# Two layers of Hedgehog linear attention and ReGLU on one core: the queries made token by token and normalised before the state products

## The chip, the cores and the metric

The kernel runs on one core of one Trainium2 chip. The metric is the device time in microseconds of one execution, as the median of the runs. The profile records one execution; its span runs from the first to the last recorded instruction.

## The reference

The input `x` has 2048 tokens of 512 features. Two layers with the same weights are applied, each an attention block A and an MLP block B, each with a layer norm without weights ahead of it and a residual behind it.

```
q, k, v = split(norm(x) @ wqkv)            # 32 heads of 16 features
p(u)    = concat(softmax(u @ w_phi), softmax(-u @ w_phi))   # 16 -> 32 features, per head
kv[h]   = sum over tokens of p(k)^T v ;  z[h] = sum over tokens of p(k)
o       = (p(q) @ kv) / (p(q) @ z + 1e-6)
x       = x + concat_heads(o) @ wo
x       = x + ((relu(norm(x) @ W_gate)) * (norm(x) @ W_up)) @ W_down      # F = 1376
```

There is no causal mask: every query needs the sums over all 2048 keys of its layer.

## The kernel before

**Tiles and stages.** The tokens form 16 tiles of 128. In each layer every tile passes through the keys (norm, transpose of the normalised tile `xn` to `xnTA`, the products K and V, the feature map of the key, and the products `kvz` that sum kv and z over all tiles). After the last tile, `build` copies the sums into `R`, the right-hand side of the state products. Then each tile passes through the attention (`attend`: state products `erq`, division, transpose of `o`, output projection `proj`, residual) and the MLP (`mlp`, in blocks of 1, 1, 2, 4, 4, 2 and 2 tiles in layer 0, and 1, 1, 2, 4, 4, 2, 1 and 1 in layer 1): gate and up products `G` and `Up` (L1068), the products of the last 96 columns `GU` (L1044), `hT` (L1076), `down` (L1101) and the residual (L1108). A finished tile of layer 0 goes on into the keys of layer 1 while other tiles are still in the MLP.

**The feature map.** The softmax over the 16 features of a head is the exponential, divided by its sum. `w_phi` is folded into the weights `Wk2` and `Wq2` at the start. For the keys, K is made token by token (128 tokens on the partitions, 512 columns); two exponentials on ACT (L852, of the value and of its negative) fill `ek`, DVE sums 64 groups of 16 (`sk`, L860), ACT makes 1/sum as exp(-ln(sum)) (L867, L870), and two halves of 512 columns are multiplied by it, on POOL or DVE (`phiK`, L879).

**The queries.** They are made feature by feature. `queries` (from L933) multiplies four tiles at once with the features on the partitions (L937), so that `Eq`, the two exponentials on ACT (L941), is already in the form that a state product needs as weights. They are not divided by their softmax sums. Instead `R` has 18 columns for each of 8 heads: 16 for kv, one for z and one of ones, masked by head. A product of 128 feature rows with 144 columns (L955) gives numerators, denominators and softmax sums; a tile needs 8 of them, in groups of 3, 3 and 2, each group in one of the two PSUM buffers of pool `q`. The copies `N` and `DS` (helper `evac`, L752 on ACT or L753 on DVE) take them out of PSUM. DVE then makes, for the softmax of the value and of the negative together: `m` (L971, L973) and its reciprocal (L975), the weights `w` (L977), the weighted numerators `pr` (L980) and their sum `o` (L985).

**From `o` to the residual.** `turn` transposes `o`, for the first two tiles of a layer on PE with a copy on ACT or DVE, for the others by a DMA transpose that SP issues (L787). Then follow `proj` (L992) and the residual sum in `X` (L997, L1001).

**The order of the work.** The order on every engine is fixed when the program is built. Each `op` is a group of instructions with an engine, a cost and a due time. `plan` is a list scheduler with modelled costs, buffers and a model of the SBUF port that DVE and POOL share. The due times (`DUE`) and the engine of the operations that can run on either of two (`PLACE`) are tables that a search has found. A buffer pool (`pool`, `psum`) has a fixed number of tiles, and an `op` that takes a buffer waits until one is free. SP issues nearly all DMAs, in its own queue order: the loads, the transposes of `xn`, `o` and `hr`, and the stores. PE gets filler products (`idle`, L746) while it would otherwise be idle near the start.

Of the kernel before, what the change touches and what calls it, by code (L numbers as in the profile page):

```python
# [8 lines left out]
P = 128  # L9
# [14 lines left out]
GE = HB * (DH + 2)  # L24
# [197 lines left out]

def dma(nbytes):
    return 530, 2000 + nbytes / RATE


class K:
# [9 lines left out]
    "1101000110000001001100001000100000000000010001111000011000010001110001000000000000011100100010111111"  # L237
    "1111000010110100000100000010000001100000011001011000011111100010000100001101010000001001111011010000"
    "1111100110100000010110000100000010100000010011011010100001000001001010001111110011001101111011000111"
    "1"  # L240
# [4 lines left out]
PAIRN, PAIRK = 4, T  # L245
# [5 lines left out]
    124840698555718, 124252925051631, 124840698555715, 125332623046249, 125332623046237, 125332623044945,  # L251
    124563716811943, 124651474002544, 125330408190868, 125332623046304, 124563716811957, 126266507667699,
    125634454115563, 126229628066192, 121775727240306, 126167001450013, 126167001450460, 127129188121561,
    127129188120464, 127094235901023, 126466639653490, 130976565015723, 126315242830809, 126026073780216,
    127094235902555, 127129188121381, 126296162928321, 126296162928067, 124164240787164, 125426364192401,
    125402334135098, 125572680463274, 125519371767392, 125974726071829, 125750504763376, 125579757280012,
    125111116517781, 125262546662859, 123870973169851, 125479091639646, 125519634893654, 125402750569735,
    125720420032606, 126315242829367, 126115429498044, 125777194724969, 125402334135128, 125288327727618,
    125426364192382, 125079834957741, 125262546664085, 125297196294117, 125083742970748, 125572680463271,
    125682458895960, 125340531910116, 125650771760537, 124924227899641, 125375805988896, 125375805988747,  # L260
    125222585690632, 124164240787379, 125079834952887, 125682458896453, 125073457285470, 124441555417783,
    125262546664362, 124559450906168, 125312265963603, 125309490505260, 125650771760388, 125521196029889,
    125302414876135, 125288971855969, 125302414876075, 125319036718893, 125310924577113, 125301244472799,
    125319889098234, 125304622980711, 124441555417022, 124696086271192, 125037102060107, 125289095968268,
    125310342882178, 125097433264852, 123938863413234, 125098635011495, 125302414877679, 125298443103361,
    125302414877834, 125345179807080, 125281974922696, 125170893464912, 125310924577844, 125298773455122,
    124760528650159, 125079834956090, 124164240787032, 125519634912639, 125297196294120, 125289095970570,
    125112530384860, 124947956071454, 125087041208877, 125295339242047, 125295339242044, 125310342881683,
    125302414876836, 125563590222055, 124550413597701, 125170893460583, 125310439811694, 125310924578485,
    125310342891023, 125079834956128, 125059086062919, 125340531910042, 125288971857093, 124938480631522,  # L270
    125016964293686, 125288327733509, 125223398503866, 125345179804453, 125223398503371, 125223398503413,
    128002429020973, 125310342881575, 125004873625443, 125004873624115, 125304250990101, 125307858833262,
    126406478372943, 124715538660738, 125381551257299, 125298773455119, 125309931740009, 125034120871986,
    125223398503145, 124934003878247, 124920547621783, 125117660356287, 125304250989589, 125381551258296,
    125724846491348, 125381551257440, 125381551255756, 124974964922671, 125098650067446, 125291692659804,
    125289095968030, 125289095968469, 125345179805242, 125288327732492, 125098635010687, 125281974923160,
    125307858833059, 125223398502787, 125307858834522, 125140858237361, 126040889629027, 125223398503832,
    125364446854524, 125252231261123, 125381551257841, 125304250990712, 125381551257935, 125172912230709,
    124370185364736, 125108599924050, 125310339518705, 125302251176246, 125291692659817, 116464344164560,
    124922363544296, 125116688267329, 125108599923765, 125310109452139, 125303189236999, 125098650066178,  # L280
    125111066291136, 125026249417504, 125310339519068, 125302251175868, 125301748943397, 125307858834419,
    125262656080157, 125307858833334, 125307858831723, 125281974922936, 125016007547146, 125096908962168,
    125140858236352, 126184070097670, 126789461067573, 124985972327150, 126493631750672, 125298443105832,
    125108599921161, 125095405692172, 124194527561572, 123915330190996, 125076395401661, 125296253501352,
    125034337760696, 125310144379949, 125172912227871, 124207139224249, 123569728375339, 125298628392740,
    125302384093186, 125034337760404, 125310109456339, 125302384093798, 124931075024483, 125294295865377,
    125294295865373, 125302251176101, 125315738277133, 125311054768224, 126406478373023, 125172912230494,
    125096908962530, 125251794872554, 124920547622585, 125303189240357, 125098650068694, 119253338445520,
    125310144376109, 124936451836160, 123979775168383, 123985197582245, 125308558845483, 125268086740942,
    125296661283390, 125310109454666, 125308302113579, 124976494725716, 125154886386050, 125154886386047,  # L290
    125310339518837, 125310339520186, 125311054773229, 115427298652791, 125028606409972, 125308302117330,
    124740066372422, 125309837287326, 124971491447171, 125390463209015, 125414317459497, 124998168317548,
    125310257912136, 125310339399315, 123124172544908, 125030291594481, 125098650066121, 125251794874681,
    125098650067377, 118590723041837, 125302384093189, 118558518521843, 119253338445444, 125315738276049,
    106461658784164, 94447193084223, 125174401625687, 125154442634399, 124740066371701, 125309837288789,
    124971491447250, 125700597007401, 125308302114021, 125724451257015, 125310339520700, 125310339519418,
    125311054772244, 106461658774504, 124207139226908, 125192403773820, 124998168316146, 125311054772195,
# [308 lines left out]
def kernel(  # L606
# [11 lines left out]
    def new(name, shape, dt=BF16):  # L618
        return sb.tile([P] + shape, dt, name=name)
# [600 lines left out]
```

## Time and profile before

| | |
|---|---|
| median of 3 runs | 383.95 us (383.95 to 384.48) |
| span of the profiled execution | 382.0 us, 7622 instructions |
| the profiled execution's own time | not given apart from its span; the median of the runs is 1.95 us above the span |
| granted TensorE clock | 1.00 in every stretch |
| PE, DVE, ACT, POOL busy | 371.5, 311.1, 215.0, 41.9 us |
| state products L955 | 256 of 128x144, 27.5 us busy |
| copies `N` and `DS` | 59 each on ACT (38.4 us), 37 each on DVE (25.0 us) |
| `m`, `m`, reciprocal, `w`, `pr`, `o` on DVE | 32 each: 6.8, 6.6, 10.9, 6.8, 21.8, 13.2 us |
| key sums `sk` on DVE | 32, 38.6 us, 1210 ns each |
| `phiK` | 38 halves on POOL (1102 ns), 26 on DVE (703 ns) |
| DMA transposes on SP | 101, landing 2.3 to 3.4 us after the issue in the median |

How to read it. Busy times of PE overlap, since a matmul is counted from its start to its modelled end, while the next one has started; the spacing of a run of matmuls in the chain of waits is their true rate. The chain of waits is followed back from the last instruction: each line has a start, a length and what ran, with a tile name and a source line. Busy time by stretches lists PE, PEld (weight loads), DVE, ACT, POOL, each with its number of instructions, then the granted clock, the share of the DMA engines and GB/s. In the timeline a line has a start, a length, the engine, the source line, the operation and the tiles, and in brackets the idle time ahead of it and what ended it.

### The profile page before, as it was taken

Reading aid. Unit: us, or ns where it says so; the run is one execution under the profiler, and the core shown is the slowest. Engines: PE = TensorE matmul, PEld = TensorE weight load, DVE = VectorE, ACT = ScalarE, POOL = GpSimd, SP = SyncE. Lnnn points to the kernel's source line nnn. Section 1 sums busy time; section 2 is a strip of 40 time slices with the busy share of each in tenths; the row PEclk is TensorE's granted clock in tenths of the full one; section 3 lists DMA queues with packets and bytes.
Section 4 is the critical chain, followed back from the end, with each engine's and each line's share of the span. In section 5 each row is a group of like instructions: output and inputs, shape, how many; then the busy total and the mean of one; then the engine's idle time right before and its main releaser. Section 6 shows DMA issues by size and latency. Waiting matters only on the chain.

```text
span 382.0 us, 7622 instructions
## 1 busy us (share of the span) xinstructions
PE 371.5 (97%) x2787; PEld 224.4 (59%) x2832; DVE 311.1 (81%) x798; ACT 215.0 (56%) x554; POOL 41.9 (11%) x44
## 2 busy tenths in 40 slices
PE   7999998999989999999999999999999999999996
PEld 4545456967545445554656654696855544467575
DVE  7999999999999989983694677999998976763334
ACT  6999989636445316772455679984526412243040
POOL 0276710000200000230020124000000000000000
PEclk9999999999999999999999999999999999999999
DMA  8497720222221321211200100013322221020110
GB/s 232 122 205 219 188 89 2 52 58 62 57 56 41 44 54 40 45 23 27 45 6 15 22 8 1 2 36 70 77 44 70 57 56 56 14 62 16 41 50 29
DMA packets 60869, 22.83 MB, mean 60 GB/s; under 512 B 52672, under 2 KB 59808, under 8 KB 60832
## 3 DMA queue, kind: packets, MB, share of 16 engines
q1 hardware_dynamic: 60416, 21.95, 24.9%
q8 instruction: 22, 0.36, 0.4%
q10 hardware_dynamic: 416, 0.39, 0.4%
q14 instruction: 15, 0.12, 0.1%
HBM read 7.91 MB, written 2.10 MB: 26 GB/s over the span
## 4 chain that ended last, share of the span: by engine, by line
PE 77%; DVE 17%; DMA 2%; issue 2%; ACT 1%; DVEq 0%
PE b L1068 31%; PE b L1101 17%; PE b L855 5%; PE b L849 5%; PE b L992 5%; PE b L937 5%; PE q L955 3%; PE b L1044 2%; PE q L896 2%; DMA xnTA<-xn 2%; DVE pr L980 1%; DVE bstA L810 1%; DVE bstB L810 1%; DVE sk L860 1%; DVE N L753 1%
## 5 line engine op out<-in xcount | busy, mean ns | idle before, releaser
L1068 PE MATMUL b<-xnTB,wgu 128*128 128x128 bf16 (+2 forms) x1191 | 152.3, 279 | 0.5
L1068 PEld LDWEIGHTS <-wgu 128*128 128x128 bf16 x1200 | 97.7, 98 | 42.5
L1072 ACT ACTIVATE gu<-b 128x512 bf16<-128x512 f32 (+1 forms) x83 | 48.0, 584 | 63.7 <-PE b L1068 61.3
L1101 PE MATMUL b<-wd,hT 128*128 128x512 bf16 (+3 forms) x349 | 82.3, 372 | 0.7
L879 POOL TENSOR_TENSOR phiK<-ek,sk 128x512 bf16<-128x512 bf16 x38 | 41.2, 1102 | 192.3 <-ACT sk L870 164.1
L1101 PEld LDWEIGHTS <-hT 128*128 128x128 bf16 (+1 forms) x363 | 34.7, 98 | 33.9 <-DVE hT L1076 0.2
L1076 DVE TENSOR_TENSOR hT<-gu 128x512 bf16<-128x512 bf16 (+1 forms) x83 | 34.0, 414 | 15.4 <-ACT gu L752 14.2
L1108 DVE SCALAR_TENSOR_TENSOR X<-b,rsB,X 128x512 bf16<-128x512 f32 (+1 forms) x33 | 23.7, 729 | 23.8 <-PE b L1101 23.8
L752 ACT CAST gu<-b 128x512 bf16<-128x512 f32 (+1 forms) x50 | 28.4, 570 | 24.0 <-PE b L1068 20.4
L860 DVE TENSOR_REDUCE sk<-ek 128x64 f32<-128x1024 bf16 x32 | 38.6, 1210 | 2.7 <-ACT ek L852 2.3
L852 ACT ACTIVATE ek<-b 128x512 bf16<-128x512 f32 x64 | 36.0, 616 | 8.3 <-PE b L849 8.1
L941 ACT ACTIVATE Eq<-b 128x512 bf16<-128x512 f32 x64 | 37.3, 629 | 3.3 <-PE b L937 3.1
L752 ACT CAST N<-q 128x384 bf16<-128x384 f32 (+1 forms) x59 | 26.1, 464 | 12.4 <-PE q L955 6.7
L855 PE MATMUL b<-wv,xnTA 128*128 128x512 bf16 x123 | 31.9, 379 | 0.3
L937 PE MATMUL b<-xnTA,Wq 128*128 128x512 bf16 x125 | 31.9, 379 | 0.2
L849 PE MATMUL b<-Wk,xnTA 128*128 128x512 bf16 x123 | 31.6, 379 | 0.4 <-DVE xnTA L753 0.2
L992 PE MATMUL b<-wo,oT 128*128 128x512 bf16 x120 | 31.3, 379 | 0.4
L753 DVE CAST gu<-b 128x512 bf16<-128x512 f32 (+1 forms) x33 | 21.8, 665 | 11.1 <-PE b L1068 11.1
L955 PE MATMUL q<-R,Eq 128*128 128x144 bf16 x256 | 27.5, 226 | 1.8 <-DVE N L753 1.3
L955 PEld LDWEIGHTS <-Eq 128*128 128x128 bf16 x256 | 20.3, 98 | 13.1 <-issue 2.6
L980 DVE TENSOR_TENSOR pr<-N,w 128x1024 bf16<-128x1024 bf16 x32 | 21.8, 683 | 0.7
L810 DVE BATCH_NORM_STATS2 bstA<-X 128x6 f32<-128x512 bf16 x32 | 21.3, 682 | 1.2 <-DMA X<-in_A_x_dram 1.0
(75 smaller groups left out, 388.9 us busy)
## 6 DMA issues: line engine op xcount, KB each, us to landing
out_dram<-X SPq DMA_DIRECT2D x15, 128.0 KB, 1.7
X<-in_A_x_dram SPq DMA_DIRECT2D x6, 256.0 KB, 3.3
wgu<-in_B_W_gate_dram SPq DMA_DIRECT2D x4, 344.0 KB, 3.4
wgu<-in_B_W_up_dram SPq DMA_DIRECT2D x4, 344.0 KB, 3.5
wd<-in_B_W_down_dram SPq DMA_DIRECT2D x5, 256.0 KB, 3.5
wv<-in_A_wqkv_dram SPq DMA_DIRECT2D x2, 256.0 KB, 4.7
wo<-in_A_wo_dram SPq DMA_DIRECT2D x4, 128.0 KB, 3.1
oT<-o SPq DMA_TRANSPOSE x28, 2.3
```

Source lines behind the costliest of these rows:

```text
L752: both = {"ACT": ("ACT", act(cols), lambda: nc.scalar.copy(out=out_(), in_=in_()), False), "DVE": ("DVE", dve(cols), lambda: nc.vector.ten ...
L849: k = op("PE", mm(4, 512), due, lambda: [nc.tensor.matmul(kp.t[:], lhsT=xnTA[c][:, b, cols], rhs=Wk2[:, b, :], start=(b == 0), stop=(b == ...
L855: v = op("PE", mm(4, 512), due_v, lambda: [nc.tensor.matmul(vp.t[:], lhsT=xnTA[c][:, b, cols], rhs=wv[:, b, :], start=(b == 0), stop=(b == ...
L860: a = op("DVE", SUM16, due, lambda: nc.vector.tensor_reduce(out=sk.t[:, row, :], in_=ek.t[:].rearrange("p g s (h f) -> p (g s h) f", f=DH) ...
L879: e.tensor_tensor(out=ph.t[:].rearrange("p g s (h f) -> p (g s h) f", f=DH)[:, lo:lo + n], in0=ek.t[:].rearrange("p g s (h f) -> p (g s h) ...
L937: q = op("PE", mm(4, 512), due(c, b), lambda b=b, qp=qp: [nc.tensor.matmul(qp.t[:], lhsT=Wq2[:, m, b * P:(b + 1) * P], rhs=xnTA[c][:, m, : ...
L941: done.append(op("ACT", act(512), due(c, b), lambda b=b, s=s, qp=qp: nc.scalar.activation(out=Eq[c][:, b, s, :], in_=qp.t[:], func=AF.Exp, ...
L955: pe.append(op("PE", mm(len(groups), GE), due, lambda ps=ps, groups=groups: [nc.tensor.matmul(ps.t[:, n * GE:(n + 1) * GE], lhsT=Eq[c][:, ...
L992: a = op("PE", mm(4, 512), due + 3, lambda: [nc.tensor.matmul(yp.t[:], lhsT=oT.t[:, b, :], rhs=wo[:, b, :], start=(b == 0), stop=(b == NB ...
L1068: nc.tensor.matmul(ps.t[:, q * W:(q + 1) * W], lhsT=wgu[:, s, b, g * P:(g + 1) * P], rhs=xT.t[:, b, 0:W], start=(b == 0), stop=(b == NB - 1))
L1072: nc.scalar.activation(out=gu.t[:, 0, 0:cols], in_=gp.t[:, 0:cols], func=AF.Relu)
L1101: nc.tensor.matmul(yp.t[:, 0:c1 - c0], lhsT=h.t[:m, f * W + i * P:f * W + (i + 1) * P], rhs=wd[:m, f, c0:c1], start=(f == 0), stop=(f == N ...
```

## The change

The queries take the way of the keys. For each tile, `query` makes Q with the tokens on the partitions (one product of 512 columns in four steps), takes two exponentials on ACT into `ek` (a tile `eq`), sums the 64 groups of 16 on DVE (`sq`), makes the reciprocals on ACT (`ln`, `exp`), multiplies two halves of 512 columns by them on POOL or DVE, and turns the result (128 tokens by 1024 features) with one DMA transpose on SP into `fq`. The state product then has 68 columns: 16 for each of 4 heads and one denominator for each. One buffer of PSUM takes all 8 products of a tile. DVE makes the reciprocal of the denominators and one multiplication from PSUM into `o`.

`R` is made by two instructions in place of eight and needs no zeros around it. The sums over the keys lie in one PSUM buffer of two banks, which is also the only buffer of the state products; before, there were two buffers of one bank. The weights `wo` load in another order of rows, in four pieces as before. `READY` lets the query sums from the third (layer 0) or fourth tile (layer 1) on be started only after the last key sum that the program lists. The tables `DUE` and `PLACE` are new throughout, so the order of all work is new. In the order of instructions of the changed kernel, DVE has 626 instructions in place of 796, 19 of the 64 halves of `eq` are on DVE and 45 on POOL; of the 64 halves of `phiK` 23 are on DVE and 41 on POOL. PE has 12 filler products in place of 13 and otherwise the same numbers of matmuls.

```diff
-GE = HB * (DH + 2)
+GE = HG * (DH + 1)
...
-    R = new("R", [2 * NB, DH + 2, HB])
+    R = new("R", [NG, GE])
-    Eq = [new(f"Eq{c}", [NB, 2, C * P]) for c in range(C)]
...
-    p_q, p_b = psum("q", 2), psum("b", 6)
+    p_q, p_b = psum("q", 1, [NG, P]), psum("b", 6, [512])
...
+    p_eq, p_sq = pool("eq", 10, [NG, 2, GQ]), pool("sq", 4, [2 * H], F32)
+    p_fq, p_rd = pool("fq", 8, [NG, P]), pool("rd", 3, [H], F32)
...
-    def queries(c, due, xT, after):
...
+    def halves(ek, out, scale, engs, due, after, takes, uses):
+        parts = []
+
+        def phi(e, lo, n):
+            e.tensor_tensor(
+                out=out().rearrange("p g s (h f) -> p (g s h) f", f=DH)[:, lo:lo + n],
+                in0=ek.t[:].rearrange("p g s (h f) -> p (g s h) f", f=DH)[:, lo:lo + n],
+                in1=scale(lo, n).unsqueeze(2).to_broadcast([P, n, DH]), op=Alu.mult)
...
+    def query(t, due, xT, behind):
         c, i = t // C, t % C
         cols = slice(i * P, (i + 1) * P)
+        qp, ek, sq, fq = Buf(p_a), Buf(p_eq), Buf(p_sq), Buf(p_fq)
+        q = op("PE", mm(4, 512), due, lambda: [nc.tensor.matmul(
+            qp.t[:], lhsT=xnTA[c][:, b, cols], rhs=Wq2[:, b, :], start=(b == 0), stop=(b == NB - 1))
+            for b in range(NB)], [xT] + q_fold, [qp, ek], name="Q")
+        e = [op("ACT", act(512), due, lambda s=s: nc.scalar.activation(
+            out=ek.t[:, :, s, :], in_=qp.t[:].rearrange("p (g e) -> p g e", e=GQ), func=AF.Exp, scale=1.0 - 2.0 * s),
+            [q], (), [qp, ek], name="Eq") for s in range(2)]
+        a = op("DVE", SUM16, due, lambda: nc.vector.tensor_reduce(
+            out=sq.t[:], in_=ek.t[:].rearrange("p g s (h f) -> p (g s h) f", f=DH), axis=AX.X, op=Alu.add),
+            e, [sq], [ek], name="sq", follow=behind)
+        a = op("ACT", RLN[0], due, lambda: nc.scalar.activation(
+            out=sq.t[:], in_=sq.t[:], func=AF.Ln, scale=1.0), [a], (), [sq], name="lnq")
+        a = op("ACT", REXP[0], due, lambda: nc.scalar.activation(
+            out=sq.t[:], in_=sq.t[:], func=AF.Exp, scale=-1.0), [a], (), [sq], name="rq")
+        a = halves(ek, lambda: ek.t[:], lambda lo, n: sq.t[:, lo:lo + n], PHI["POOL"], due, [a], [], [ek, sq])
+        a = op("SP", XWIDE, due, lambda: nc.sync.dma_start_transpose(
+            out=fq.t[:], in_=ek.t[:].rearrange("p g s e -> p (g s e)")), a, [fq], [ek], name="fq", move=1000)
+        return fq, a
...
+    def attend(l, t, due, made_q, made, how):
+        fq, ready = made_q
+        rd, o, oT, yp, ps = (Buf(p) for p in (p_rd, p_o, p_oT, p_a, p_q))
+        pe = [op("PE", SUMS, due, lambda: [nc.tensor.matmul(
+            ps.t[:, g, 0:GE], lhsT=fq.t[:, g, :], rhs=R[:, g, :], start=True, stop=True) for g in range(NG)],
+            [ready] + made, [ps], [fq], name="erq")]
+        a = op("DVE", rcp(32), due, lambda: nc.vector.reciprocal(
+            out=rd.t[:].rearrange("p (g j) -> p g j", j=HG), in_=ps.t[:, :, GQ:GE]), pe, [rd], [ps], name="rden")
+        a = op("DVE", dve(512), due, lambda: nc.vector.tensor_tensor(
+            out=o.t[:].rearrange("p (g j d) -> p g j d", g=NG, d=DH),
+            in0=ps.t[:, :, 0:GQ].rearrange("p g (j d) -> p g j d", d=DH),
+            in1=rd.t[:].rearrange("p (g j) -> p g j", g=NG).unsqueeze(3).to_broadcast([P, NG, HG, DH]),
+            op=Alu.mult), [a], [o], [ps, rd], name="o")
         a = turn(o, lambda: oT.t[:], how, due, a, [oT], [], "oT", split=SPLIT)
...
-        eq = [queries(c, lambda c, b: TL[l] - 14000 + p["QS"] * c + 850 * b, xT[c * C:(c + 1) * C], eq_free[c]) for c in range(C)]
+        eq = [query(t, TL[l] - 14000 + p["QS"] / 4 * t, xT[t], keys.sk[-1:] if t >= READY[l] else []) for t in range(T)]
```

## The prediction

> **What bounds the kernel now.** I read the busy times first, then the three stretches (0 to 55 us layer 0's keys, 55 to 130 its attention and first MLP blocks, the rest), then the chain of waits, and last the timeline where POOL and DVE run together.
>
> ```profile
> PE 371.5 (97%) x2787; PEld 224.4 (59%) x2832; DVE 311.1 (81%) x798; ACT 215.0 (56%) x554; POOL 41.9 (11%) x44
> ```
>
> Busy time by stretches:
>
> ```profile
> 0.00:55.00 55.00, 52.36 (x383) 27.05 (x391) 50.91 (x106) 49.00 (x133) 23.91 (x28) 1.00 0.71 183
> 55.00:130.00 75.00, 72.13 (x602) 47.18 (x609) 72.99 (x230) 44.40 (x121) 2.12 (x2) 1.00 0.22 44
> 130.00:382.00 252.00, 247.01 (x1805) 150.22 (x1833) 187.25 (x464) 121.57 (x301) 15.84 (x14) 1.00 0.17 37
> ```
>
> After the stretch and its length come PE, PEld, DVE, ACT, POOL. PE looks full everywhere, but a pipelined matmul counts too long. DVE is full up to 130 us (97% in the second stretch) and free afterwards. So there are two bounds: DVE's queue to about 130 us, PE's from there.
>
> The chain of waits gives PE's true spacing (start, length, what):
>
> ```profile
> 30.44 0.86 PE b L937 x4
> 31.31 0.26 PE q L896 x8
> ...
> 55.61 0.20 PE q L955 x3
> ...
> 184.39 0.43 PE b L1101 x2
> ...
> 185.26 0.87 PE b L1068 x8
> ...
> 247.55 0.89 PE b L1068 x16
> ```
>
> One matmul of 512 columns takes 0.216 us, of 256 0.109, of 144 0.0625, of 128 0.056, of 65 0.0325; 192 lies at 0.083. Counted in PE's queue: 1173 x 0.2158 + 422 x 0.1092 + 128 x 0.0825 + 584 x 0.0558 + 256 x 0.0625 + 256 x 0.0325 + 13 fillers x 0.2158 = 369.5 us. In the span of 382.0 PE therefore loses 12.5 us. Where:
>
> ```profile
> 124.58 0.41 DVE L985 TENSOR_TENSOR o<-pr 128x512 bf16<-128x512 bf16 x1
> 128.68 1.04 PE L992 MATMUL b<-wo,oT 128*128 128x512 bf16 x4
> 131.95 0.41 DVE L985 TENSOR_TENSOR o<-pr 128x512 bf16<-128x512 bf16 x1
> 141.01 1.03 PE L992 MATMUL b<-wo,oT 128*128 128x512 bf16 x4
> ```
>
> These are `o` and output projection of layer 0's thirteenth and fifteenth tile. From `o` to projection through the DMA transpose: 124.99 to 128.68, 3.7 us. Ahead of the fifteenth projection PE has 132.4 us of work and starts it at 141.0: 8.6 of the 12.5 us are lost by then, behind DVE (ahead of the thirteenth, 120.1 us of work, it is already 8.6). The other 3.9 come later, mostly in the tail.
>
> **PE's part.** 256 products of 144 columns become 256 of 68. Nearest row is the key sum, 65 columns with a weight load each, 0.26 us for 8: I take 0.0325 for 68 as well. 256 x 0.030 = 7.7 us, one filler less 0.2: PE's work becomes 361.6 us. Bounds: 68 columns at the slope of the other rows are no dearer than 0.0325; at the 128-column row (0.056) only 1.7 us would be saved.
>
> The Trainium skill speaks against this ("TensorE: Matmul & The Clock Gate", Back-to-back issue gap): in a stream of weight load and matmul it gives about 81 ns for 128 columns, the load being part of it. By that the narrower product saves nothing, 7.7 us less than forecast. The rows of 33 and 56 ns, each with its load, contradict it, and I go by them.
>
> **DVE's part, to the fifteenth `o`.** I compare both queues up to the same point, counting a DVE instruction at its mean less 0.06 us, the overlap with the next one (a key sum, 1210 ns, occupies 1.13 us of the chain; an `N` copy, 546 ns, 0.47).
>
> Added: 18 query reductions `sq` (16 tiles and two of layer 1) at 1.13 as `sk`: 20.3. 11 halves of `eq` scaled on DVE at 0.62 (`phiK` on DVE, 678 ns in the early stretch): 6.8. 15 `rden` and new `o`, the second waiting for the first: 0.34 as `m L975`, and 0.61 as L1001 (512 columns with a PSUM operand): 14.3. Two more key sums that the new order puts ahead: 2.3. Likewise put ahead are a statistics (0.62), four aggregates (0.4), an `xn` (0.33), an `hT` (0.33), an MLP residual (0.69) and, counted against a weight copy that leaves, one copy (0.62): 3.0. Together 46.7.
>
> Removed: 21 copies of `N` (15 x 0.49, 6 x 0.34) and 21 of `DS` (0.14, 0.12): 12.2. Two `phiK`: 1.2. The eight pieces of R and its memset against two instructions: 1.7. And 15 times `m`, `m`, `rden`, `w`, `pr`, `o`: 213 + 205 + 342 + 213 + 683 + 413 = 2.07 us where they wait for each other, 1.71 where other work fills in: 25.6 to 31.0. Together 40.7 to 46.1.
>
> DVE reaches the fifteenth `o` 0.6 to 6.0 us later; I take 3.3. It shows first at R: between the last key sum and R the new queue holds three products (3 x 0.62) and three query reductions (3 x 1.13), 5.3 us, while the last `kvz` needs less; nothing on PE covers it, for the next in PE's queue is `erq`.
>
> **POOL beside DVE.** `eq` brings 45 halves to POOL and `phiK` three more, 48 x 1.10 = 53 us; about 24 of them, 26 us, run while DVE is the bound. What this does to DVE the timeline shows where `phiK` ran late:
>
> ```profile
> 161.78 0.92 DVE L1076 TENSOR_TENSOR hT<-gu 128x512 bf16<-128x512 bf16 x1 [0.28 <-ACT gu L752]
> 166.76 1.22 DVE L1022 TENSOR_SCALAR xn<-X,mvB 128x512 bf16<-128x512 bf16 x1
> 170.95 0.75 DVE L1076 TENSOR_TENSOR hT<-gu 128x512 bf16<-128x512 bf16 x1 [0.45 <-ACT gu L752]
> ...
> 159.68 2.74 POOL L879 TENSOR_TENSOR phiK<-ek,sk 128x512 bf16<-128x512 bf16 x2 [56.09 <-ACT sk L870]
> 165.77 2.07 POOL L879 TENSOR_TENSOR phiK<-ek,sk 128x512 bf16<-128x512 bf16 x2 [3.35 <-DVE X L1001]
> 170.27 1.14 POOL L879 TENSOR_TENSOR phiK<-ek,sk 128x512 bf16<-128x512 bf16 x1 [2.43 <-ACT sk L870]
> ```
>
> Alone, `hT` takes 0.42 and `xn` 0.35. Here they lasted until POOL's instruction ended: 0.50 + 0.87 + 0.33 = 1.7 us lost in 5.95 us of POOL, 0.29 per us. In the stretch 27 to 55, with 15.9 us of POOL, `xn` (398) and `phiK` on DVE (678) were not stretched at all. So 26 us of POOL cost 0 to 7.6 us; I take 2, nearer the early stretch, which like the new one has both engines full, with DVE mostly at work (`sq`, `o` from PSUM, statistics) of kinds that no row shows stretched.
>
> The Trainium skill has this too ("GPSIMD Engine Reference", Key points): the two engines share SBUF interfaces, and contend when DVE runs in a 2-port mode or with two SBUF inputs. It gives no price, and the early stretch shows that it need not happen.
>
> **What is covered.** ACT loses the other `N` and `DS` (38.4 us) and gains 64 short `ln` and `exp` at 0.28 (18 us); it binds nothing. SP issues 32 wide transposes; the narrow ones hold SP 1.2 us and land after 2.3, so these cost 38 to 77 us of a mostly idle queue. Behind them stand the transposes of `o`, `xn` and `hr`. Four wide ones lie ahead of the first `oT`, whose seven POOL halves (7.7 us) run beside R and the first two tiles' `o`; if that cover goes, the third tile waits about 3 us. The weights of `wo` load in the same four pieces: 0.
>
> The two PSUM banks are now one buffer: `erq` of a tile waits for `o` of the tile before. In the middle MLP matmuls fill the 1.5 us. At the start of layer 1 (`erq`, `rden`, `o`, transpose on PE, ACT's copy, projection) the cover ahead of the first projection shrinks from 5.9 us of PE work to 1.6: +1 us (0 to 2).
>
> **The sum.** DVE's fifteenth `o` ends at 132.4 + 3.3 + 2 = 137.7, its projection can start at 141.4. PE has 128.7 us of work ahead of it (444 of 512 columns, 80 of 256, 32 of 192, 240 of 128, 120 of 68, 128 of 65), so 12.7 us are lost by then, against 8.6. Then 3.9 as before and 1 for layer 1: 361.6 + 12.7 + 3.9 + 1.0 = 379.2 us of span, 2.8 less. Around the span lie 383.95 - 382.0 = 1.95 us (the median of the three runs against the span, the profiled execution's own time not being given apart): **381.1 us**. So 7.9 us leave PE, and about 5 come back as waiting for DVE.
>
> **Rivals.**
> - *The saving arrives whole.* DVE comes out even (its low end) and POOL costs nothing: PE loses 12.5 us as before: 361.6 + 12.5 + 1.95 = 376.1. For it: 170 DVE instructions fewer (796 to 626). Against: R is behind three reductions whatever the prices. 0.13.
> - *POOL's traffic stretches DVE, and it is slower.* Place: 55 to 140 us, `hT`, `xn` and `eq` on DVE beside `eq` on POOL. Full price 7.6 instead of 2: 386.7. It decides from 4.9 us (2 + 2.85 of gain), that is 17 of the 26 us of POOL at 0.29. For it: the lines above; against: the early stretch. 0.22.
> - *The query chain is late.* `Q`, two exponentials, `sq`, `ln`, `exp`, two halves on POOL (2.2), wide transpose: `erq` waits about 1.5 us in each layer, DVE behind it: 384. Against: the first two tiles are ready early. 0.08.
> - The forecast, 379 to 383.5: 0.57.
>
> **How the numbers follow.** A measurement here tells about 0.2% (0.8 us) from no change. The forecast's upper edge gives 0.04 to "same", the POOL case 0.04, the late chain 0.02; slower are 0.18 + 0.06; faster are 0.53 + 0.13. So 0.66, 0.10, 0.24. The range 377 to 386.5 leaves out part of the first rival and POOL's extreme.
>
> **What would show it.** Right: `erq` 0.26 us for 8 in the chain; R starts 3 to 5 us after 52.5; DVE full until about 138; fifteenth projection near 141 to 142; PE unstalled after. Wrong: 68 columns above 0.04 us; R at 53 and PE's loss at the fifteenth projection still 9 (first rival); `hT` or `xn` at 0.9 to 1.2 us between 55 and 140 (POOL); `erq` released by the wide transpose (late chain).

## The result and the profile after

The changed kernel takes **388.54 us** (387.84 to 389.48, 4 runs) against 383.95 (383.79 to 384.48): ratio 1.0122 [1.0104, 1.0139], 4.6 us slower. Forecast were 381.1 us, with a range to 386.5. The profiled execution of the changed kernel has a span of 387.1 us and 388.88 us in all.

Busy times and the granted clock by slices, from its page:

```profile
PE 370.3 (96%) x2831; PEld 218.4 (56%) x2831; DVE 314.8 (81%) x628; ACT 202.1 (52%) x503; POOL 92.6 (24%) x92
...
PEclk9999995999999999999999999999999999999999
```

Busy time by the same three stretches as before (length, then PE, PEld, DVE, ACT, POOL, clock, DMA share, GB/s):

```profile
0.00:55.00 55.00, 50.72 (x352) 26.10 (x352) 51.14 (x93) 48.21 (x134) 28.81 (x32) 1.00 0.79 193
55.00:130.00 75.00, 67.82 (x606) 43.57 (x607) 72.95 (x151) 37.33 (x100) 25.62 (x24) 0.93 0.55 96
130.00:387.00 257.00, 251.76 (x1875) 148.77 (x1873) 190.67 (x386) 116.57 (x272) 38.20 (x36) 1.00 0.28 52
```

DVE is as full as before up to 130 us, PE is not (67.8 of 75 instead of 72.1), POOL has twice the work, and the clock falls. The chain of waits shows where PE stood:

```profile
53.58 1.20 DVE sk L602
54.78 2.66 DVE phiK L622 x3
57.45 3.38 DVE sq L689 x3
60.93 0.61 DVE R L651
61.58 0.63 PE q L705 x8
62.23 0.37 DVE rd L708
62.62 0.70 DVE o L710
...
64.66 1.89 PE b L716 x4
...
91.01 0.26 PE q L705 x8
```

DVE's queue at the same place before, from the timeline (the second of the two `sk` starts at 47.93):

```profile
46.81 2.34 DVE L860 TENSOR_REDUCE sk<-ek 128x64 f32<-128x1024 bf16 x2
49.07 3.09 DVE L879 TENSOR_TENSOR phiK<-ek,sk 128x512 bf16<-128x512 bf16 x5
52.52 0.37 DVE L924 SCALAR_TENSOR_TENSOR R<-q,Mf 64x16 bf16<-64x16 f32 x2 [0.36 <-PE q L896]
```

The last key sum `sk` starts at 53.58 us, 5.6 us later than before. `R` stands behind three `phiK` and three query sums, so it starts at 60.8, 8.3 us later than before. PE has nothing queued ahead of the first state products. Afterwards even its own work is slow: the projection of 4 x 512 columns takes 1.89 us, twice its 0.86, and the eight narrow products 0.63, where they take 0.26 later on; the granted clock is down to half there (its rows stand in the last section).

Call **loss** what the prediction took for PE's account: the time at which PE reaches a point of its queue, less the work queued ahead of it at full clock. All kernels below are read this way:

| loss at | 55 us | 70 | 100 | 150 | 225 | 330 |
|---|---|---|---|---|---|---|
| before | 4.8 | 7.2 | 7.1 | 8.4 | 8.3 | 9.0 |
| changed | 7.1 | 16.9 | 17.8 | 18.6 | 18.4 | 21.9 |

The work fell by 7.9 us (369.5 to 361.6) and the loss rose by 13: 2.3 by 55 us, 7.4 between 55 and 70, 2.8 in layer 1 from 225 to 330 us.

The fifteenth `o` of layer 0 and its projection, from the timeline, answer to the pair shown of before (131.95 and 141.01):

```profile
140.76 0.68 DVE L710 TENSOR_TENSOR o<-q,rd 128x512 bf16<-128x512 f32 x1
...
147.29 1.03 PE L716 MATMUL b<-wo,oT 128*128 128x512 bf16 x4
```

And an `xn` of the key stage of the changed kernel beside POOL. It ends at 33.18, just behind the first of POOL's two halves (31.98 and half of 2.12 make 33.04); without POOL beside it, it takes 0.40:

```profile
31.98 2.12 POOL L622 TENSOR_TENSOR phiK<-ek,sk 128x512 bf16<-128x512 bf16 x2 [0.65 <-ACT sk L613]
32.02 1.16 DVE L567 TENSOR_SCALAR xn<-X,mvA,rsA 128x512 bf16<-128x512 bf16 x1
```

### The profile page after: what moved, and what is told of

It is laid out like the page before. It is cut to its first block, busy times and chain, and to the rows that moved or that the text cites. A ratio compares the mean times of both kernels' runs of the same rounds, so it can differ in the third digit from the quotient of the medians.

```text
span 387.1 us, 7573 instructions
## 1 busy us (share of the span) xinstructions
PE 370.3 (96%) x2831; PEld 218.4 (56%) x2831; DVE 314.8 (81%) x628; ACT 202.1 (52%) x503; POOL 92.6 (24%) x92
## 4 chain that ended last, share of the span: by engine, by line
PE 60%; DVE 23%; DMA 6%; ACT 5%; issue 4%; SPq 1%; DVEq 0%; ACTq 0%
PE b L792 28%; PE b L825 16%; PE b L716 4%; DVE sq L689 4%; DVE sk L602 3%; DMA fq<-eq 3%; PE b L591 3%; PE b L597 2%; DVE o L710 2%; PE b L768 2%; DVE bstB L552 2%; DVE xn L567 2%; PE q L705 1%; DMA X<-in_A_x_dram 1%; ACT eq L686 1%
## 5 line engine op out<-in xcount | busy, mean ns | idle before, releaser
L792 PE MATMUL b<-xnTB,wgu 128*128 128x128 bf16 (+2 forms) x1200 | 147.2, 279 | 0.0
L825 PE MATMUL b<-wd,hT 128*128 128x512 bf16 (+2 forms) x363 | 83.8, 372 | 0.0
L622 POOL TENSOR_TENSOR phiK<-ek,sk 128x512 bf16<-128x512 bf16 x41 | 44.6, 1108 | 106.4 <-ACT sk L613 65.4
L667 POOL TENSOR_TENSOR eq<-eq,sq 128x512 bf16<-128x512 bf16 x45 | 47.4, 1077 | 92.0 <-ACT sq L694 83.0
L686 ACT ACTIVATE eq<-b 128x512 bf16<-128x512 f32 x64 | 36.1, 605 | 16.5 <-PE b L683 16.3
L494 ACT CAST gu<-b 128x512 bf16<-128x512 f32 (+1 forms) x53 | 30.2, 569 | 19.3 <-PE b L792 18.9
L689 DVE TENSOR_REDUCE sq<-eq 128x64 f32<-128x1024 bf16 x32 | 38.1, 1204 | 0.0
L716 PE MATMUL b<-wo,oT 128*128 128x512 bf16 x128 | 33.7, 387 | 1.1 <-ACT oT L494 0.6
L683 PE MATMUL b<-Wq,xnTA 128*128 128x512 bf16 x128 | 32.5, 380 | 0.5 <-DMA xnTA<-xn 0.5
L710 DVE TENSOR_TENSOR o<-q,rd 128x512 bf16<-128x512 f32 x32 | 21.7, 680 | 0.2
L552 DVE BATCH_NORM_STATS2 bstB<-X 128x6 f32<-128x512 bf16 x32 | 21.4, 676 | 0.2
```

The costliest lines, as they stand in the source:

```text
L552: a = op("DVE", STATS, due, lambda: nc.vector.bn_stats(out=bst[:, t, :], in_=x_of(t)), after, name="stats")
L622: e.tensor_tensor(out=ph.t[:].rearrange("p g s (h f) -> p (g s h) f", f=DH)[:, lo:lo + n], in0=ek.t[:].rearrange("p g s (h f) -> p (g s h) ...
L667: e.tensor_tensor(out=out().rearrange("p g s (h f) -> p (g s h) f", f=DH)[:, lo:lo + n], in0=ek.t[:].rearrange("p g s (h f) -> p (g s h) f ...
L686: e = [op("ACT", act(512), due, lambda s=s: nc.scalar.activation(out=ek.t[:, :, s, :], in_=qp.t[:].rearrange("p (g e) -> p g e", e=GQ), fu ...
L689: a = op("DVE", SUM16, due, lambda: nc.vector.tensor_reduce(out=sq.t[:], in_=ek.t[:].rearrange("p g s (h f) -> p (g s h) f", f=DH), axis=A ...
L716: a = op("PE", mm(4, 512), due + 3, lambda: [nc.tensor.matmul(yp.t[:], lhsT=oT.t[:, b, :], rhs=wo[:, b, :], start=(b == 0), stop=(b == NB ...
```

## The experiments

Sixteen of the runs have 3 rounds, the last has 5; each time is a median, with the ratio to the kernel before run beside it. Base is the changed kernel unless another is named. "Moved" means another place in the order that the planner wrote; a number in brackets is a tile: sq(11) is the query sum of tile 11.

### 1. Two query chains later

```diff
-DVE: ... phiK x3, sq(11), sq(14), sq(3), Rz, R, ...
+DVE: ... phiK x3, sq(3), Rz, R, ... sq(11), sq(14) ten instructions on
```

> The query chains of tiles 11 and 14 (sum, ln, exp, two halves, transpose) move from just before R of layer 0 to about ten DVE instructions behind it; nothing else moves. Theory A (PE runs empty between the last key products and R because R stands behind DVE work that nobody needs yet, and the clock halves after that): R starts at 58.9 to 59.1 us, released by the last key product, instead of 60.85; PE's loss at 70 us falls from 16.9 to about 14.5; time 386.0 to 386.6 against 388.5. Rival B (DVE is the bound as far as the fifteenth tile, so work moved behind R only delays the tiles after it): R earlier, but loss at 140 us again 18, time 388.5.

**393.71 us**, 1.0253 [1.0236, 1.0270]. The expectation at R held (loss at 70 us 14.3), but PE then lost 4.6 us at once:

```profile
75.64 0.64 PE L705 MATMUL q<-R,fq 128*128 128x68 bf16 x8 [4.64 <-DMA fq<-eq]
```

The tiles are not attended in the order of their numbers but as 0, 1, 2, 3, 11, 7, 14, 6, 12, 4, 5, and so on. The chain of tile 11 was the one due next. The edit moved the wrong chains; it shows that a late chain costs PE directly.

### 2. Fillers for the clock

```diff
+busy = {kvz(last): 4, erq(first): 11, oT(first): 4}   # products of zeros, 512 columns
```

> 19 matmuls of zeros (0.216 us each, 4.1 us), into a PSUM bank that nobody uses then, go into PE's queue where it stood empty: 4 before the last key product, 11 before the first erq, 4 before the first turn of o. They are shorter than the gaps. Theory A says that the granted clock fell to 0.50 from 58 to 66 us because PE was nearly empty before: with the fillers 1.00 throughout, the first two projections at 0.87 us instead of 1.9, time 386.0 (2.5 less). If the clock falls for another reason it still shows 0.50 there, and the time is 388.5 or more; if PE waits for DVE there anyway, the clock recovers and the time is still 388.5.

**389.14 us**, 1.0129 [1.0086, 1.0172]. In the profiled execution the clock was 1.00 throughout, and the first projection took 1.04 us instead of 1.89:

```profile
63.27 1.04 PE L716 MATMUL b<-wo,oT 128*128 128x512 bf16 x4 [0.42 <-ACT oT L494]
```

So it was the emptiness of PE that let the clock fall, and work without use held it. But the median did not fall. The two executions at a clock of 1.00 took 387.42 and 387.94 us, some 0.9 less than the changed kernel; the two at 0.995 and 0.996 took 391.05 and 390.34. Most of the half clock lies in time that PE would spend waiting.

### 3. Short POOL halves ahead of R

```diff
-"POOL": phi(nc.gpsimd, k * H, H)
+"POOL": phi(nc.gpsimd, k * H, 4)      # until R of layer 0, phiK and eq
```

> POOL's halves of phiK and eq ahead of R of layer 0 scale 4 heads of 32 instead of 32, so POOL works some 5 us instead of 28.8 in the first 55 us; the rest of those halves stays unscaled. DVE's instructions are the same. Theory C (POOL stretches DVE in the key stage, xn and phiK by 3.8 us): no xn above 0.45 us, the last key sum starts at 50 instead of 53.6, the wait of 1.6 us for a turned tile at 37.8 us is gone, R starts at 57 or before, time 383.5 to 385. If the key stage is late for another reason (DVE's own added work): last key sum still at 53 to 53.6, time 388 to 388.5.

The other 28 of the 32 heads of such a half stay unscaled; the run leaves this work out.

**385.93 us**, 1.0052 [1.0029, 1.0076]: 2.6 us gained, with DVE's instructions unchanged. DVE's groups up to 58 us (busy, mean ns), of the kernel before, of the changed one, and of this run:

```profile
L879 DVE TENSOR_TENSOR phiK<-ek,sk 128x512 bf16<-128x512 bf16 x10 | 6.5, 678 | 0.0
L825 DVE TENSOR_SCALAR xn<-X,mvA,rsA 128x512 bf16<-128x512 bf16 x16 | 6.1, 400 | 0.6 <-ACT rsA L820 0.6
```
```profile
L567 DVE TENSOR_SCALAR xn<-X,mvA,rsA 128x512 bf16<-128x512 bf16 x16 | 8.4, 551 | 0.6 <-ACT rsA L562 0.6
L622 DVE TENSOR_TENSOR phiK<-ek,sk 128x512 bf16<-128x512 bf16 x8 | 7.4, 954 | 0.0
```
```profile
L567 DVE TENSOR_SCALAR xn<-X,mvA,rsA 128x512 bf16<-128x512 bf16 x16 | 6.1, 403 | 0.7 <-ACT rsA L562 0.6
L622 DVE TENSOR_TENSOR phiK<-ek,sk 128x512 bf16<-128x512 bf16 x8 | 5.3, 688 | 0.0
```

The same `xn` takes 400 ns before, 551 changed, 403 with POOL short; `phiK` 678, 954, 688. The stretching is 2.3 + 2.1 = 4.4 us ahead of R. Not all of it was on the path: the last key sum came 1.5 us earlier (52.05), not the 3.6 that I expected; R came at 58.4, 2.4 earlier. The wait of 1.6 us for a turned tile at 37.8 us shrank to some 0.2. Up to the last key sum DVE was busy 46.5 us instead of 49.8 (44.4 before), but it also stood idle 1.7 us longer, mostly for the loads of `X`. What is left of its lateness against the kernel before is, for the larger part, three query sums (3.6 us) that the new order puts ahead of it.

### 4. State products of 128 columns

```diff
-rhs=R[:, g, :]                       # 68 columns
+rhs=R[:, g * GE:g * GE + P]          # 128 columns
```

> The 256 products of the normalised queries with R read 128 columns instead of 68 (the next group's columns, not used). By the rows at 0.0558 and 0.0325 us each costs 0.023 us more, 6.0 us in all. If PE is the bound from 72 us on and the narrow product is what was saved: erq 0.45 us for 8 instead of 0.26, time 394 to 394.5. If the narrow product costs no less than one of 128 columns, or PE has slack there (DVE or the transposes bound): within 1 us of 388.5.

**393.99 us**, 1.0254 [1.0239, 1.0269]: 5.45 us more, 21 ns a product where 23 were forecast; eight take 0.45 us in the chain instead of 0.26. PE's side of the forecast holds, against the rule of equal gaps that was weighed there: the column is paid for, and what leaves PE's queue leaves the time.

### 5, 6, 7. R first, query products as cover, both

```diff
-DVE: phiK x3, sq(11), sq(14), sq(3), Rz, R, rden, o, sq(7), ..., sq(5), ..., sq(12)
+DVE: phiK x3, sq(3), Rz, R, rden, o, sq(11), ..., sq(7), ..., sq(14)     # 5: (12), (5) still later
+PE:  Q(13) ahead of the first erq, Q(9) ahead of the first turn of o     # 6
```

> As in the run with the two chains moved, R of layer 0 stands behind one query sum instead of three, but now the chains follow in the order in which their tiles are attended (2, 3, 11, 7, 14, then 6, 12, 4, 5): each later sum takes the place of the next one, and those of tiles 5 and 12, needed last, move back. Theory A (the waits at R are the loss, and DVE has time later): R at 58.9 to 59.3 us, PE's loss at 70 us 14.3 and at 140 us 15.5 to 16 (18.5 in the changed kernel), no wait for a query's transpose at 75 us, time 385.7 to 386.5. Rival B (DVE is the bound to the last tile of layer 0): loss at 140 us 18 to 18.5 again, time 388.5.

> Two query products of later tiles (four matmuls of 0.216 us each) are moved forward in PE's queue: tile 13's ahead of the first erq, tile 9's ahead of the first turn of o, where PE waits 2.8 and 1.2 us. Nothing else moves. Theory A: work is done in the empty time, 1.7 us less loss at 70 us (15.2), and the clock comes back sooner or does not fall as far (0 to 1 us more); time 385.8 to 386.8. Rival: their places later were needed as cover for the transposes of the first tiles, and the wait only moves to 66 to 72 us: 388 to 388.5.

> Both edits together. Theory A: the two gains overlap in the wait ahead of the first erq (0.9 us of it is left with R earlier, which one product fills): loss at 70 us 12.5 to 13, time 384 to 385. Rival B: 388 to 388.5.

**389.13** [1.0101, 1.0155], **389.35** [1.0107, 1.0169] and **389.55 us** [1.0119, 1.0164]: none is faster than the changed kernel. With both edits R starts at 58.5, the clock stays at 1.00 in the profiled execution, and PE reaches 65 us with a loss of 11.8 instead of 15.4. By 100 us it is 17.5 again. What PE waited for between 54 and 100 us there (us in total, times, longest):

```profile
PE q L639 <- DVE phiK L622: 2.2, 3, 1.2
PE b L539 <- DVE xn L742: 1.9, 1, 1.9
PE b L716 <- DMA oT<-o: 1.3, 1, 1.3
PE b L825 <- DVE hT L800: 1.2, 2, 0.6
...
```

My first theory, that the waits at R were the cause and DVE had time later, falls here: the gain was given back. Two suspects are in the list: DVE's queue (`xn`, `hT`), and a transpose on SP.

### 8. Short POOL halves behind R

```diff
-"POOL": phi(nc.gpsimd, k * H, H)
+"POOL": phi(nc.gpsimd, k * H, 4)      # eq only, from R of layer 0 on
```

> From R of layer 0 on, the query halves on POOL scale 4 heads of 32 (the rest of them stays unscaled); DVE's instructions are the same. The prediction put 2 us (0 to 7.6) on POOL beside DVE from 55 to 140 us. Theory A (PE waits for DVE nowhere between 72 and 150 us but for 1.5 us in all): loss at 150 us 17 to 18.5 instead of 18.6, and in layer 1, where the query chain is late by 0.5 to 0.8 us twice, 1 to 1.5 us less: time 386 to 388. Rival (POOL stretches DVE and DVE is the bound through 140 us): loss at 150 us 14 to 16, time below 385.

**387.82 us**, 1.0095 [1.0072, 1.0118]: 0.7 less than the changed kernel, as long as R is late. That is within the scatter (386.74 to 388.65 here, 387.84 to 389.48 there).

### 9. Query sums short behind R

```diff
 # base: both edits of run 7
-in_=...[:, :, 0:DH]
+in_=...[:, :, 0:2]        # sq, from R of layer 0 on: 2 of the 16 values, 0.27 us instead of 1.20
```

> Base: R first and two query products as cover (both edits). From R of layer 0 on, the query sums read 2 of 16 values (normalisers wrong), so that each takes about 0.2 us of DVE instead of 1.13; everything else stays. With both edits PE reached 65 us with a loss of 11.8 us, and gave 5.7 back by 100 us. Theory B (DVE is full from 60 to 100 us, and PE waits there for DVE's work whatever its order): the gain stays, loss at 100 us 12 to 13.5 instead of 17.5; in layer 1, too, the loss between 225 and 330 us (3.6) falls to 1 to 2; time 380 to 383. Rival D (the later waits come from the new places of the transposes and products, not from DVE's amount of work): loss at 100 us still 16 or more, time 386 to 388.

**387.73 us**, 1.0093 [1.0063, 1.0122]: only 1.8 less than with both edits. DVE now had time: it was busy for 4.62 of the 10 us from 70 to 80. Yet the loss at 100 us was 18.8. The timeline (lines picked out, in the order of their starts) says why:

```profile
61.15 7.72 SPq L697 DMA_TRANSPOSE fq<-eq  x4
...
63.47 4.14 POOL L667 TENSOR_TENSOR eq<-eq,sq 128x512 bf16<-128x512 bf16 x4 [0.31 <-ACT sq L694]
...
65.57 0.67 DVE L710 TENSOR_TENSOR o<-q,rd 128x512 bf16<-128x512 f32 x1
...
68.96 3.42 SPq L529 DMA_TRANSPOSE oT<-o  x2
...
72.98 1.29 PE L716 MATMUL b<-wo,oT 128*128 128x512 bf16 x4 [2.34 <-DMA oT<-o]
```

The third tile's `o` is ready at 66.24, but its transpose is issued at 68.96: SP stands at the fourth wide transpose, which waits for POOL's halves (done at 67.61). PE's projection waits 2.34 us for it. So DVE's amount of work was not all; the lateness of POOL's results reaches PE through SP's queue as well.

### 10, 11. Reciprocals, then PSUM copies, from DVE to ACT

```diff
 # base: both edits
-nc.vector.reciprocal(out=rd, in_=den)
+nc.scalar.activation(out=rd, in_=den, func=Ln); nc.scalar.activation(out=rd, in_=rd, func=Exp, scale=-1)
+# 11: copies of up-projections and of turned MLP inputs, DVE -> ACT
```

> Base: both edits. The reciprocal of the denominators is made on ACT as exp of minus ln for tiles 2 to 15 of both layers (two instructions of about 0.27 us, 0.2 us longer than DVE's 0.36 us); nothing is left out. DVE loses 14 x 0.30 = 4.2 us by the end of layer 0's attention, 2.4 of it by 100 us. Theory B: loss at 100 us 15 to 16 instead of 17.5, time 386 to 387.5 where both edits alone gave 389.55. Rival D: 389.5, or slower by the longer chain.

> As the run before, and DVE's copies of up-projections and turned MLP inputs from PSUM go to ACT too, where they stand in the same place of the order (0.6 us each, five of them in layer 0). Nothing is left out. Theory B: 2 us more than the run before, partly, for ACT must be in time: 384.5 to 387. Rival D: no less than the run before.

**390.52** [1.0140, 1.0212] and **389.97 us** [1.0095, 1.0207]: no gain. In run 10 the loss at 100 us was 17.6 as with both edits, and in layer 1 it rose by 4.2 instead of 3.6. Taking some 4 us from DVE in this way brings nothing; the two instructions on ACT also make each tile's chain some 0.2 us longer, so the run does not price DVE's work alone.

### 12. All POOL halves short

```diff
 # base: both edits
-"POOL": phi(nc.gpsimd, k * H, H)
+"POOL": phi(nc.gpsimd, k * H, 4)      # phiK and eq, both layers
```

> Base: both edits. All halves on POOL, phiK and eq, in both layers scale 4 heads of 32 (the rest stays unscaled); DVE's instructions are the same. Short halves ahead of R alone took 2.6 us, behind R alone 0.7. Theory B (DVE is the bound, stretched by POOL): DVE's last o of layer 0 some 5 us earlier, loss at 100 us 12.5 to 14.5, time 382 to 385. Rival D: 386 to 388.

**382.15 us**, 0.9946 [0.9927, 0.9965]: 7.4 less than with both edits, the only kernel here below the one before. DVE is full from 60 to 100 us all the same (busy by stretches, columns as above):

```profile
60.00:70.00 10.00, 8.22 (x115) 6.28 (x112) 10.00 (x20) 7.92 (x21) 1.09 (x4) 1.00 0.51 99
70.00:80.00 10.00, 9.18 (x126) 7.39 (x126) 10.00 (x21) 4.26 (x13) 1.09 (x4) 1.00 0.49 82
...
90.00:100.00 10.00, 9.86 (x83) 6.75 (x81) 10.00 (x25) 5.09 (x14) 0.90 (x3) 1.00 0.63 113
```

The loss at 100 us is 12.2, at 150 12.6, at 330 14.5. With the same instructions DVE is busy 305.2 us in the whole execution, not 315.5 as in run 7. Runs 3 and 8 gained 2.6 and 0.7, together 3.3; both at once with R moved forward gain 7.4. This fits with a price ahead of R and one behind it that hid each other; no run has all halves short without R moved forward.

Runs 9 and 12 together give a hint by which way POOL costs time behind R. From 65 to 100 us the loss rises by 5.7 us with both edits, by 6.2 in run 9, where DVE's instructions are 24 us shorter in the whole execution (291.3 instead of 315.5), and by 2.2 here, where they are 10 us shorter and POOL's 62 (30.2 instead of 92.6). That speaks for the lateness of POOL's results more than for DVE's busy time. It is not a proof: R is also 3.3 us earlier here than in run 7 (55.2 and 58.5).

### 13. One transpose later in SP's queue

```diff
 # base: both edits
-SP: fq(2), fq(3), fq(11), fq(7), oT(2), oT(3)
+SP: fq(2), fq(3), fq(11), oT(2), fq(7), oT(3)
```

> Base: R first and two products as cover (389.55, loss 11.8 at 65 us and 17.5 at 100). One wide transpose, of the query of the sixth tile attended, moves from just ahead of the third tile's transpose of o in SP's queue to just behind it; nothing else. There SP stood until 68.2 us, waiting for POOL's halves of that query, while that o was done at 66.1. Theory E (the late transposes on SP, behind POOL, give the gain back): the transpose of o is issued at 66.2, the wait of 1.3 us at 72.3 is gone, loss at 100 us about 16, time 388 to 388.6. Theory B (DVE): the same time goes into waits for xn and hT, loss at 100 us 17 to 17.5, time 389.2 to 389.7.

**388.78 us**, 1.0128 [1.0101, 1.0154], 0.8 less than with both edits, within the scatter. The wait of 1.3 us at 72.3 is gone, but the loss at 100 us is 18.1: PE waits 1.9 us for DVE's `xn`, and 0.9 each for DVE's `o` and for the transposes of queries. SP's order is real but only the first of several limits at nearly the same height.

### 14. Short halves with other POOL work behind each

```diff
 # base: run 3
+nc.gpsimd.tensor_tensor(out=scratch[28 heads], in0=scratch, in1=idle)   # behind each short half
```

> The changed kernel with POOL's halves ahead of R cut to 4 heads of 32 (385.93 when only that was done), and each followed by a multiplication of 28 heads on a tile that nobody reads, so that POOL works and moves as much as before but its results are ready up to 0.8 us earlier. If POOL costs by stretching DVE (xn and phiK of the key stage): xn at 0.7 to 1.2 us again, last key sum at 53 to 53.6, time 388 to 388.8. If it costs by the lateness of its results: time 385.5 to 386.5.

**388.24 us**, 1.0113 [1.0093, 1.0133]: 2.3 of the 2.6 us are back. The edit gave POOL not the same work as in the changed kernel but more: it was busy 37.5 us up to 55 us, against 28.8 there and 12.4 in run 3. The last two halves ahead of R end at 55.7 and 57.3 us; in the changed kernel at 56.9 and 58.4, in run 3 at 55.2 and 55.5. So they come earlier than in the one and later than in the other. The profile supports the stretching only in part: `phiK` is stretched again, `xn` hardly, and the loss at 70 us is 15.9, midway between 14.7 and 16.9. The run shows that POOL's time ahead of R costs; it does not show by which way.

```profile
L624 DVE TENSOR_TENSOR phiK<-ek,sk 128x512 bf16<-128x512 bf16 x8 | 6.6, 858 | 0.0
L569 DVE TENSOR_SCALAR xn<-X,mvA,rsA 128x512 bf16<-128x512 bf16 x16 | 6.6, 432 | 1.0 <-ACT rsA L564 1.0
```

### 15, 16, 17. Scaling one half only, and better orders

A factor common to both softmaxes of a query's head cancels in numerator over denominator. So only the ratio of the two sums is needed, and one product of 512 columns instead of two; nothing is left out.

```diff
-sq = exp(-ln(sq));  eq[half 0] *= sq;  eq[half 1] *= sq
+sq[neg] = exp(-ln(sq[neg])) * sq[pos];  eq[neg] *= sq[neg]
 # 16: with both edits and 13.  17: also the last phiK halves exchanged between POOL and DVE, sq(2), sq(3) behind them
```

> The changed kernel, correct and whole: a query needs only the ratio of its two sums per head, since a factor common to both halves cancels in numerator over denominator. ACT's ln and exp work on 32 columns, POOL multiplies 32 columns (0.2 us), and one product of 512 columns scales the second half, where it was two. 32 instructions leave (some 23 on POOL at 1.06 us, 9 on DVE at 0.65). The order is as it was. If POOL's halves are the price: time 385.5 to 387.5, the rest being R's place. If they are not: 388.5.

> One half scaled, with R first, two products as cover, and the SP order of this batch's first run; correct and whole. With short halves everywhere the two edits gave 382.15; phiK keeps its POOL halves here (3 us of price ahead of R). Expected 384 to 386; DVE has 6 us less to do, which may bring it to 383.

> Base: one half scaled with the three order edits (386.87). Near R: two of DVE's last three phiK halves go to POOL, which stood idle from 52.3 to 54.8 us, and POOL's very last one goes to DVE; the query sums of tiles 2 and 3 move behind the last key sum and behind R; the second tile's centring moves ahead of the third tile's o (PE waited 1.3 us for it). Whole and correct. If R's place still counts: R at 55.5 to 56.5 us instead of 58.0, PE's loss at 70 us 11.5 instead of 13.5 and at 150 us 14 to 14.5 instead of 16, time 384.5 to 385.5, at best level with the kernel before. If the gain is given back again by DVE's queue behind R: 386.5 to 387.

**389.14** [1.0116, 1.0146], **386.87** [1.0061, 1.0094] and **386.48 us** [1.0046, 1.0074]. By itself the smaller scaling gains nothing, and neither does the order; together they gain 1.7 us against the changed kernel (2.1 with run 17's order). POOL is then busy 77.6 us instead of 92.6. The loss of run 16 is 13.5 at 70 us and 16.0 at 150. In run 17 R came at 57.5, not at 55.5 to 56.5, since the last key products now waited for POOL; its loss, 14.4 at 70 us and 16.8 at 150, is no lower than run 16's, so the 0.4 us between the two are not shown to come from R's place. It is the best whole version found, and still 0.6% slower than the kernel before.

## Why the prediction was wrong

**PE's part was right.** 7.9 us less work, 0.26 us for eight products; run 4 gives 60 columns a price of 5.45 us against the 6.0 of the row used.

**DVE's count was right, POOL's stretching was not.** Up to the end of the fifteenth `o` of layer 0 DVE was busy 126.3 us before and 135.5 after: 9.2 us more, and that `o` ends at 141.4 instead of the forecast 137.7. The counted terms came out well: 18 query sums 20.2 us (20.3), 11 halves 7.0 (6.8), reciprocals and `o` 13.6 (14.3), the copies removed 11.5 (12.2), the chain of six removed 26.0 (25.6 to 31.0). In run 12, with POOL short, the queue to the same point is busy 129.7 us, 3.4 more than before: the 3.3 of the sum. What failed is the term **"POOL beside DVE", taken at 2 us**. Against the same instructions of run 12, those of the changed kernel are some 6 us longer to that point: `xn` 2.7, `phiK` 2.1, `eq` 0.6, `hT` 0.6.

The mistake has a place. I priced only the POOL work that lies between 55 and 140 us, and took for it the row of the early stretch, where POOL was busy 24 us without harm. Just there, in the key stage, the new order with 28.8 us of POOL lost 4.4 us on DVE. That two engines have run side by side unharmed in one order is no price for another order: whether a DVE instruction meets a POOL instruction depends on where each falls. The rows at 0.92 and 1.22 us were the better ones to go by, though not in full: at their 0.29 the 56.7 us of POOL up to that point would have cost 16 us.

**R.** Forecast 3 to 5 us after 52.5; it was 8.3. The 5.3 us from the last key sum to R were right (6.0, one `phiK` being stretched by 0.9); that the key sum itself would come 5.6 us late was not in the sum. The three query sums ahead of it were counted as DVE work up to the fifteenth `o`, but not in R's time, and the stretching of `xn` and `phiK` ahead of it was put at nothing. Nor was the falling clock in the sum.

**How DVE's lateness becomes time.** This path was wrong too. The forecast let the fifteenth `o` decide. That `o` ended at 141.4, its transpose was issued at 143.5 and landed at 145.9, and its projection started at 147.3 without a wait, when PE's queue came to it: PE had lost 17.8 us by 100 us, 9.8 of them between 55 and 70 us, around R. At this projection the loss was 18.6 instead of the 12.7 of the forecast, behind it 6.9 instead of 4.9; together that is the whole miss of 7.9 us in the span (387.1 instead of 379.2).

Runs 5 to 7, 9 and 13 show that R is not alone. Ahead of about 100 us, R, DVE's `xn` and `hT`, POOL's chains and SP's order seem to lie within 1 to 2 us of each other: where one was relieved, the next took the gain. The prediction's own remark on cover, that the third tile would wait about 3 us for its `oT` behind four wide transposes if the cover went, is what runs 7 and 9 show, 1.3 and 2.3 us.

**Layer 1** was put at +1 us; the loss from 225 to 330 us rose by 3.5 instead of 0.7, in six steps of 0.4 to 0.65 us, where PE waits for a turned `o`, its copy, a query's transpose, `xnTA` or, twice, DVE's `o`. With POOL short it rose by 1.9. The rest of this is not settled.

**The rivals.** "POOL's traffic stretches DVE" (386.7, chance 0.22) had the right sign, and its stretching is in the rows, with the place too late; that the time was lost by this way alone is not shown. "The query chain is late" (0.08) is small in the changed kernel, 0.6 us of waiting for turned queries up to 100 us, and 4.6 us at once in run 1. "The saving arrives whole" (376.1) needed DVE even and POOL free; run 12, with POOL nearly free and R moved forward, stands at 382.15, only 2 us faster than before.

What stays open: no run parts the stretching of DVE from the lateness of POOL's results. And the four or more executions of one changed kernel scatter by up to 5 us (run 11: 387.7 to 393.1), those of the kernel before by less than 2. In runs 2, 7, 11 and 13 the executions at a lower granted clock are the longer ones (run 13: 387.9 and 388.6 at 1.00, 389.0 at 0.996, 390.5 at 0.991), in runs 8 and 17 they are not; which of the two is the cause no run shows.

## What to carry to other kernels

Price POOL work beside DVE over the whole stretch in which DVE is the bound, with every collision as one end of the range and the quiet row only as the other; here some 6 us were measured between 0 and 16. Ask also who waits for POOL's results. In an order that a search has tuned, several limits stand at nearly the same height: an early gain at one of them proves nothing until PE's loss is read again 30 us later. Where a wait is cured, look at who stands behind whom in the in-order queues, SP's above all.

## What the runs showed of the hardware

**DVE beside POOL.** In the key stage of the changed kernel five of the 16 `xn` (from SBUF to SBUF) and three of the first eight `phiK` (two SBUF operands) were held up. `xn` ended about 0.15 us behind POOL's instruction, `phiK` about 0.55 us behind it: up to 1.16 and 1.54 us instead of 0.40 and 0.68. `sk` and `sq`, which only reduce, keep a mean of 1.20 us in every run, but for the shortened sums of run 9. The Trainium skill ("SBUF — State Buffer", Who interferes with whom) says the same: one port pair, held for a whole instruction, the loser blocked, reductions never. Between runs 7 and 12, 10.3 us came off DVE's busy time (315.5 to 305.2) when POOL's fell from 92.6 to 30.2: 0.17 us for each us of POOL taken away, a little over half of the 0.29 of the prediction's worst rows.

**The clock.** With PE busy for 0.80 to 0.95 us of each 2 us from 54 to 60 us, the granted clock, as a mean of 2 us, went to 0.81 at 56 to 58, 0.50 from 58 to 66 and 0.63 at 66 to 68. The Trainium skill ("TensorE: Matmul & The Clock Gate", Part 1: The HAM clock gate) tells of a half rate after an idle window of about 3.4 us. Here the clock fell at 57.24 us, before PE had waited longer than 1.2 us at a time; being busy for some 40% of the 3.4 us ahead of it was not enough to hold it. The half rate lasted 10.24 us, in run 3 6.83 and in runs 10 and 16 3.41: each a multiple of 3.41 us, so the length of the window agrees.

```profile
56.00:58.00 2.00, 0.80 (x14) 0.68 (x15) 2.00 (x2) 1.08 (x4) 2.00 (x2) 0.81 0.00 0
58.00:60.00 2.00, 0.82 (x15) 0.70 (x13) 2.00 (x3) 0.77 (x3) 1.13 (x2) 0.50 0.02 4
...
64.00:66.00 2.00, 1.78 (x12) 0.79 (x10) 1.94 (x4) 1.00 (x3) 2.00 (x3) 0.50 0.67 128
```

At 64 to 66 us PE is nearly full and still at half rate; it is back at 1.00 at 68.
